# Down sums of three token blocks with stationary weights and transposed results, and V of the first 512 tokens moved ahead of wide Q and K projections

## The chip, the cores and the metric

The kernel runs on one core of a Trainium2 chip. The metric is the device time of one execution in microseconds (us), as a median over several runs. A profile, where one was taken, gives the *span*: from the first to the last instruction of the program on the core. The timed figure is longer than the span in every run here, by 1.73 to 2.14 us; that difference turns out to matter here.

Each run also lists the granted clock, the share of TensorE's full clock that the chip allowed.

## The reference, cut to what matters

```python
S, D, F, H, W, dil = 2048, 640, 1536, 32, 8, 2        # bf16 in and out
xn  = layernorm(x)
q, k, v = split(xn @ wqkv)                            # 640 -> 3 x 640
o   = local attention: each token looks at 8 tokens, 2 apart, per head of 20
out = x + o @ wo + ((xn @ w_gate) * (xn @ w_up)) @ w_down
```

## The kernel before: the parts that matter here

The kernel keeps everything of the 2048 tokens on the chip. Tokens come in 16 tiles of 128 and in 4 blocks of 512. `XNT` holds the normalized input with features on partitions. TensorE runs one long in-order list: Q and K of tiles 0 to 7, Q and K of blocks 2 and 3, V of blocks 0 to 3, gate and up ("GLU") of blocks 0 to 2, down of block 0, GLU of block 3, down of blocks 1 to 3. VectorE does LayerNorm, then the attention products, the softmax and the weighted sums of V, and leaves the attention output in `VO`. The down sum of a token adds 12 chunks of the GLU product (weights `WD`) and 5 chunks of `VO` (weights `WO`): 17 matmuls that accumulate in one PSUM bank.

Q and K of tiles 4 and 5 are computed one tile at a time (128 columns in a matmul), those of tiles 2, 3, 6 and 7 two tiles at a time (256 columns), because LayerNorm delivers tiles one after the other:

```python
def proj_part(which, t, ms, b, col):                  # 128 wide
    for c, m in [(c, m) for m in ms for c in range(NCH)]:
        o = PS[:, b, col + (m - ms[0]) * TS:col + (m - ms[0] + 1) * TS]
        l, x = wcols(which, c, m), XNT[:, c, t * TS:(t + 1) * TS]
        ...                                           # matmul, accumulating over c
def proj_wide(which, t0, m, b, col):                  # 256 wide
    o = PS[:, b, col:col + 2 * TS]
    ...
wide_pair(2)                                          # tiles 2, 3
for which, t in ((0, 4), (1, 4), (0, 5), (1, 5)):
    proj_part(which, t, (0, 1), b, 0); proj_part(which, t, (2, 3), b, 2 * TS); proj_part(which, t, (4,), ...)
wide_pair(6)                                          # tiles 6, 7
```

The down sum holds the activations stationary and streams the weights, 320 of the 640 output features at a time, so the result comes out with tokens on partitions and can be added to the output in memory as it is:

```python
def tail(t, nb):                                      # one tile of 128 tokens, one half of the features
    for i in range(n):                                # n = 12 + 5 = 17
        if i < NF: l, x = ht(j, i)[:, rows], WD[:, i, cols]                       # cols: 320 features
        else:      l, x = VO[:, i - NF, t * TS:(t + 1) * TS], WO[:, i - NF, cols]
        op("pe", ... matmul(PS[:, b, 0:wid], l, x, start=(i == 0), stop=(i == n - 1)))
    if t < TLAST:                                     # tiles 0 to 11: ScalarE evicts 640 features as fp16,
        ...                                           # and for every 2 tiles a DMA of the POOL queue adds them to `out`
    # tiles 12 to 15: VectorE adds x, plain DMA to `out`
```

## Time and profile before

| | |
|---|---|
| timed, 3 runs | 254.13 us median (253.92 to 254.18) |
| the profiled run | 376.75 us, span 375.0 us, granted clock 0.658 |

The profile fell into a throttled run, so its microseconds aren't those of the timed runs. The view of the cores says so:

```profile
core 0: 375.0 us, clock 0.658
```

The page of the same profile, its busy times and its clock line (tenths of full speed in 40 equal slices of the span):

```profile
PE 371.7 (99%) x1572; PEld 184.2 (49%) x1572; DVE 219.0 (58%) x255; ACT 114.5 (31%) x202; POOL 35.8 (10%) x44
...
PEclk8666666666666666666666666666666666666666
```

TensorE (PE) is busy all the time. What a slice of that time consists of is seen in the chain of waits, the work that ended last followed back. Its columns are start, length in us, and engine, tile and line with the number of instructions. L509, L489 and L474 are projections 256, 128 and 512 wide, L648 is GLU, L679 the down sums:

```profile
15.24 8.19 PE PS L509 x50
23.43 8.12 PE PS L489 x100
31.56 8.19 PE PS L509 x50
39.75 65.25 PE PS L474 x200
105.00 117.50 PE PS L648 x360
222.50 27.81 PE PS L679 x136
250.31 39.17 PE PS L648 x120
289.48 83.23 PE PS L679 x425
```

The pieces follow each other without a gap. Divide a length by its count and by the width: 8.12 us / 100 / 128 = 0.634 ns a column at a width of 128, 65.25 / 200 / 512 = 0.637 at a width of 512. At this clock a narrow matmul costs no more per column than a wide one, so this profile alone can't show what widening is worth.

The new gate of the change is on `VO`, which VectorE writes. In the timeline of the same profile (start, length, engine, line, operation), a 256-token piece of it takes from 236.60 to 247.36 us:

```profile
236.60 5.49 DVE L615 TENSOR_TENSOR PVB<-VO,ATB 128x10240 f16<-128x10240 bf16 x1
242.12 4.35 DVE L610 TENSOR_TENSOR PVB<-PVB 128x5120 f16<-128x5120 f16 x2
246.50 0.82 DVE L610 TENSOR_TENSOR VO<-PVB 128x1280 bf16<-128x1280 f16 x1
247.36 5.49 DVE L615 TENSOR_TENSOR PVB<-VO,ATB 128x10240 f16<-128x10240 bf16 x1
```

### The profile page before, as it was taken

The numbers are of one execution on the slowest core, as the hardware profiler recorded it, in microseconds if no ns is written. First come the engines' busy times: TensorE is split into PE (matmuls) and PEld (weight loads), VectorE is DVE, ScalarE is ACT, GpSimd is POOL, SyncE is SP. The second block draws the span as 40 slices with busy tenths as digits, with TensorE's granted clock in tenths as the row PEclk, the third lists the DMA queues.
The fourth block names the chain that finished last, engine by engine and source line by source line (L and its number), as shares of the span: only waits on it lengthen the run. The fifth ranks groups of instructions, "written<-read, shape, count | busy, mean of one in ns | idle before, by whom it ended". The sixth has DMA issues, their size and how long they took to land.

```text
span 375.0 us, 3825 instructions
## 1 busy us (share of the span) xinstructions
PE 371.7 (99%) x1572; PEld 184.2 (49%) x1572; DVE 219.0 (58%) x255; ACT 114.5 (31%) x202; POOL 35.8 (10%) x44
## 2 busy tenths in 40 slices
PE   8999999999999999999999999999999999999997
PEld 5998544444433333333333346553334556556555
DVE  5766899992017238967666432997846998000111
ACT  4544443333333344333333332113333001001000
POOL 0000012344000300111100000110000010010000
PEclk8666666666666666666666666666666666666666
DMA  7754696766100412453991000612000020220411
GB/s 218 217 115 84 181 361 148 129 120 120 20 0 2 92 20 82 149 107 71 251 344 18 0 1 0 180 80 35 2 0 0 0 37 0 35 37 0 72 35 35
DMA packets 25664, 31.83 MB, mean 85 GB/s; under 512 B 9872, under 2 KB 22160, under 8 KB 25616
## 3 DMA queue, kind: packets, MB, share of 16 engines
q1 hardware_dynamic: 19120, 22.16, 18.3%
q0 software_dynamic: 6240, 9.31, 15.7%
q8 instruction: 12, 0.20, 0.2%
q10 hardware_dynamic: 288, 0.13, 0.1%
q14 instruction: 4, 0.03, 0.0%
HBM read 14.42 MB, written 4.59 MB: 51 GB/s over the span
## 4 chain that ended last, share of the span: by engine, by line
PE 99%; DVE 0%; issue 0%
PE PS L648 42%; PE PS L679 30%; PE PS L474 17%; PE PS L509 4%; PE PS L502 2%; PE PS L489 2%; PE PS L452 1%; PE PS L433 0%; DVE FOUT L693 0%; DVE ZERO L296 0%; DVE EPSC L297 0%
## 5 line engine op out<-in xcount | busy, mean ns | idle before, releaser
L648 PE MATMUL PS<-XNT,WU 128*128 128x512 bf16 x240 | 87.3, 513 | 0.0
L648 PE MATMUL PS<-XNT,WG 128*128 128x512 bf16 x240 | 87.3, 513 | 0.0
L474 PE MATMUL PS<-XNT,WQKV 128*128 128x512 bf16 x200 | 65.4, 513 | 0.0
L679 PE MATMUL PS<-WD,HT 128*128 128x320 bf16 (+2 forms) x300 | 63.4, 382 | 0.0
L648 PEld LDWEIGHTS PS<-XNT,WG 128*128 128x128 bf16 x240 | 29.3, 122 | 48.8 <-issue 48.7
L648 PEld LDWEIGHTS PS<-XNT,WU 128*128 128x128 bf16 x240 | 29.0, 121 | 49.3 <-issue 49.3
L679 PEld LDWEIGHTS PS<-WD,HT 128*128 128x128 bf16 x300 | 35.5, 120 | 24.1 <-issue 0.9
L653 DVE TENSOR_TENSOR HT<-HT,USX 128x512 bf16<-128x512 bf16 x36 | 15.2, 422 | 54.8 <-ACT USX L650 54.8
L474 PEld LDWEIGHTS PS<-XNT,WQKV 128*128 128x128 bf16 x200 | 26.9, 135 | 38.0 <-issue 37.7
L615 DVE TENSOR_TENSOR PVB<-VO,ATB 128x10240 f16<-128x10240 bf16 x8 | 43.9, 5488 | 0.2
L650 ACT ACTIVATE USX<-PS 128x512 bf16<-128x512 f32 x48 | 28.6, 597 | 48.7 <-PE PS L648 47.7
L679 PE MATMUL PS<-WO,VO 128*128 128x320 bf16 (+2 forms) x165 | 38.8, 384 | 0.0
L610 DVE TENSOR_TENSOR PVB<-PVB 128x5120 f16<-128x5120 f16 (+1 forms) x16 | 34.5, 2155 | 0.3
L693 DVE TENSOR_TENSOR FOUT<-PS,XR 128x320 bf16<-128x320 f32 (+2 forms) x9 | 4.1, 454 | 51.7 <-PE PS L679 51.7
L650 ACT ACTIVATE HT<-PS 128x512 bf16<-128x512 f32 x36 | 21.5, 597 | 36.4 <-PE PS L648 36.4
L688 ACT ACTIVATE FACC<-PS 128x640 f16<-128x640 f32 x12 | 8.4, 703 | 73.3 <-PE PS L679 73.3
L543 POOL DMA_DIRECT2D LOG<-PE x24 | 21.9, 925 | 58.0 <-DMA LOG<-PE 58.0
L679 PEld LDWEIGHTS PS<-WO,VO 128*128 128x128 bf16 x165 | 19.7, 121 | 13.0
L703 POOL DMA_DIRECT2D out_dram<-FACC x6 | 7.1, 1186 | 141.9 <-ACT FACC L688 141.9
L532 DVE TENSOR_TENSOR PP<-QH,KH 128x2048 f16<-128x2048 bf16 x16 | 19.1, 1218 | 0.0
L532 DVE TENSOR_TENSOR TMP<-QH,KH 128x2048 f16<-128x2048 bf16 x16 | 19.0, 1218 | 0.0
L537 DVE TENSOR_TENSOR PP<-PP,TMP 128x4096 f16<-128x4096 f16 x8 | 18.3, 2289 | 0.2
(67 smaller groups left out, 250.6 us busy)
## 6 DMA issues: line engine op xcount, KB each, us to landing
PE<-PP POOLq DMA_DIRECT2D x8, 512.0 KB, 4.8
ATB<-LOG SPq DMA_DIRECT2D x8, 512.0 KB, 4.8
LOG<-PE POOLq DMA_DIRECT2D x24, 128.0 KB, 2.7
WG<-in_B_w_gate_dram SPq DMA_DIRECT2D x1, 1920.0 KB, 9.1
WU<-in_B_w_up_dram SPq DMA_DIRECT2D x1, 1920.0 KB, 15.8
WD<-in_B_w_down_dram SPq DMA_DIRECT2D x1, 1920.0 KB, 10.0
out_dram<-in_A_x_dram SPq DMA_DIRECT2D x1, 1920.0 KB, 9.1
out_dram<-FACC POOLq DMA_DIRECT2D x6, 320.0 KB, 4.8
```

The costliest lines, as they stand in the source:

```text
L474: op("pe", (lambda l, x, c: lambda e: e.matmul(PS[:, b, :], l, x, start=(c == 0), stop=(c == NCH - 1)))(l, x, c), r=[l, x], w=[PS[:, b, :] ...
L509: op("pe", (lambda l, x, c: lambda e: e.matmul(o, l, x, start=(c == 0), stop=(c == NCH - 1)))(l, x, c), r=[l, x], w=[o], name=f"pw{which}_ ...
L532: return (1.22, lambda: op("dve", lambda e: e.tensor_tensor(o, qw, kw, ALU.mult), r=[q, k], w=[o], name=f"prod{h}_{p}_{c}"))
L537: (2.3, lambda: op("dve", lambda e: e.tensor_tensor(a, a, b, ALU.add), r=[a, b], w=[a], name=f"psum{h}_{p}")),
L543: op("pool", lambda e: e.dma_start(o, i, accum_op=ALU.add), r=[o, i], w=[o], dma=True, name=name)
L610: return lambda: op("dve", lambda e: e.tensor_tensor(o, x, y, ALU.add), r=[x, y], w=[o], name=f"{name}_{b}")
L615: lambda: op("dve", lambda e: e.tensor_tensor(PVB[:], vw, aw, ALU.mult), r=[v, a], w=[PVB[:]], name=f"pv_{b}")),
L648: op("pe", (lambda l, x, c: lambda e: e.matmul(PS[:, b, :], l, x, start=(c == 0), stop=(c == NCH - 1)))(l, x, c), r=[l, x], w=[PS[:, b, :] ...
L650: op("act", lambda e: e.activation(o, PS[:, b, :], ACT.Copy), r=[PS[:, b, :]], w=[o], name=f"guev{which}_{m}_{j}")
L653: h_pending.append(lambda: op("dve", lambda e: e.tensor_tensor(h, h, o, ALU.mult), r=[h, o], w=[h], name=f"h{m}_{j}"))
L679: op("pe", (lambda l, x, i, b, wid: lambda e: e.matmul(PS[:, b, 0:wid], l, x, start=(i == 0), stop=(i == n - 1)))(l, x, i, b, wid), r=[l, ...
L688: op("act", (lambda o, i: lambda e: e.activation(o, i, ACT.Copy))(o, i), r=[PS[:, b - 1, :], PS[:, b, :]], w=[o], name=f"fin{t}")
```

## The change

The intent: the same columns in fewer, wider matmuls. For blocks 0 to 2 the down sum keeps the *weights* stationary and streams 512 tokens; the result then has features on partitions, so ScalarE writes it to `DT`, and a DMA of the sync queue transposes it into `FACC`, from where it is added to the output as before. Q and K of tiles 4 to 7 become one block of 512 columns. Since all four tiles must be there before the first such matmul, V of the first 512 tokens is put ahead of them, and V's weights are loaded earlier.

```diff
+    def down_t(j, d):                                   # block j, output features d*128 .. d*128+127
+        for i in range(n):                              # n = 17
+            if i < NF: l, x = WD[:, i, cols], ht(j, i)
+            else:      l, x = WO[:, i - NF, cols], VO[:, i - NF, toks]       # 512 tokens
+            op("pe", ... matmul(PS[:, b, :], l, x, start=(i == 0), stop=(i == n - 1)))
+        o = DT[:, (NCH * j + d) % 4]
+        op("act", ... activation(o, PS[:, b, :], ACT.Copy))
+        f = FACC[j][:, :, cols]
+        op("sp", lambda e: e.dma_start_transpose(f, o), r=[o], w=[f], dma=True)
+        ...                                             # after d == 4: two accumulating DMAs to `out`, 256 tokens each
     x_load2(8)
+    wqkv_load(2)                                        # V's weights, before: with the late loads
     x_load2(10)
...
-    wide_pair(2); (tiles 4 and 5 by proj_part); wide_pair(6)
+    (tiles 2 and 3 as before)
+    for m in range(NCH):
+        proj(2, m, 0)                                   # V of block 0
+    for m in (4, 0, 1, 2, 3):
+        for which in (0, 1):
+            proj(which, m, 1)                           # Q, K of block 1: 512 wide
...
     def add_dn(j):
+        if j < NJ - 1:
+            for d in range(NCH):
+                fill.append(("dn", 2 * j + 1, 3.67, lambda d=d: down_t(j, d)))
+            return
```

More of the change, by code (lines that the diff above doesn't have):

```diff
@@ L274, in build_kernel @@
     FOUT = sb("FOUT", [128, NFO, D])
-    FACC = sb("FACC", [128, NFO, D], FP16, at=place[0] - NFO * D * 2)
+    DT = sb("DT", [128, 4, JB], FP16, at=K.base[ATB[1].name] + NSB * W * SB * 2)
+    FACC = [sb(f"FACC{k}", [128, NJ, D], FP16, at=a) for k, a in
+            enumerate((place[0] - NFO * D * 2, K.base[ATB[0].name], K.base[ATB[0].name] + NJ * D * 2))]
     NUS = 7
@@ L343, in late_loads @@
         dma(MASK[0:128:4], MSK0[0:32], r=[MSK0[0:32]], w=[MASK[0:128:4]], name="mask")
-        wqkv_load(2)
         for T, src in ((WG, B_w_gate), (WU, B_w_up)):
@@ L482, in proj @@
            name=f"pev{which}_{m}_{j}")
-    def proj_part(which, t, ms, b, col):
-        for c, m in [(c, m) for m in ms for c in range(NCH)]:
-            o = PS[:, b, col + (m - ms[0]) * TS:col + (m - ms[0] + 1) * TS]
-            l, x = wcols(which, c, m), XNT[:, c, t * TS:(t + 1) * TS]
-            st, sp = c == 0, c == NCH - 1
-            op("pe", (lambda o, l, x, st, sp: lambda e: e.matmul(o, l, x, start=st, stop=sp))(o, l, x, st, sp),
-               r=[l, x], w=[o], name=f"pp{which}_{m}_{t}_{c}")
     def proj_tile(which, tiles, bm, at={}):
@@ L661, in build_kernel @@
     stores = []
-    fin_bank = [0]
+    def down_t(j, d):
+        flush_h(0)
+        b = bank()
+        n = NF + NCH
+        cols, toks = slice(d * TS, (d + 1) * TS), slice(j * JB, (j + 1) * JB)
+        for i in range(n):
+            if i < NF:
+                l, x = WD[:, i, cols], ht(j, i)
+            else:
+                l, x = WO[:, i - NF, cols], VO[:, i - NF, toks]
+            op("pe", (lambda l, x, i: lambda e: e.matmul(PS[:, b, :], l, x, start=(i == 0), stop=(i == n - 1)))(l, x, i),
+               r=[l, x], w=[PS[:, b, :]], name=f"dt{j}_{d}_{i}")
+        o = DT[:, (NCH * j + d) % 4]
+        op("act", lambda e: e.activation(o, PS[:, b, :], ACT.Copy), r=[PS[:, b, :]], w=[o], name=f"fin{j}_{d}")
+        f = FACC[j][:, :, cols]
+        op("sp", lambda e: e.dma_start_transpose(f, o), r=[o], w=[f], dma=True, name=f"oT{j}_{d}")
+        if d < NCH - 1:
+            return
+        for u in range(0, NJ, 2):
+            f2 = FACC[j][:, u:u + 2]
+            t = NJ * j + u
+            h = ohbm[t * TS:(t + 2) * TS, :].rearrange("(u p) n -> p u n", p=TS)
+            stores.append(op("pool", (lambda h, f2: lambda e: e.dma_start(h, f2, accum_op=ALU.add))(h, f2), r=[f2, ("out",)],
+                             w=[("out", t)], dma=True, name=f"oacc{t}"))
     def tail(t, nb):
@@ L680, in tail @@
                    r=[l, x], w=[PS[:, b, :]], name=f"dn{t}_{nb}_{i}")
-            if t < TLAST:
-                if nb == 0:
-                    fin_bank[0] = b
-                    continue
-                assert b == fin_bank[0] + 1
-                o = FACC[:, t % NFO, :].rearrange("p (n d) -> p n d", n=2)
-                i = PS[:, b - 1:b + 1, 0:wid]
-                op("act", (lambda o, i: lambda e: e.activation(o, i, ACT.Copy))(o, i),
-                   r=[PS[:, b - 1, :], PS[:, b, :]], w=[o], name=f"fin{t}")
-                continue
             o = FOUT[:, t % NFO, cols]
@@ L697, in tail @@
                 stores.append(dma(ohbm[t * TS:(t + 1) * TS, cols], o, r=[o], name=f"odma{t}_{c0}", eng=eng))
-        if nb == 1 and t < TLAST:
-            if t % 2 == 0:
-                return
-            f = FACC[:, (t - 1) % NFO:(t - 1) % NFO + 2, :]
-            d = ohbm[(t - 1) * TS:(t + 1) * TS, :].rearrange("(u p) n -> p u n", p=TS)
-            stores.append(op("pool", lambda e: e.dma_start(d, f, accum_op=ALU.add), r=[f, ("out",)], w=[("out", t)],
-                             dma=True, name=f"oacc{t}"))
-        elif nb == 1 and not last:
+        if nb == 1 and not last:
             f = FOUT[:, t % NFO, :]
@@ L772, in build_kernel @@
     tp = 11.9
-    def wide_pair(t0):
-        nonlocal tp
-        for g in range(5):
-            b = bank()
-            if g == 2:
-                proj_wide(0, t0, 4, b, 0)
-                proj_wide(1, t0, 4, b, 2 * TS)
-                part_evac(0, t0, 2, 4, 1, b, 0)
-                part_evac(1, t0, 2, 4, 1, b, 2 * TS)
-            else:
-                which, m = ((0, 0), (0, 2), None, (1, 0), (1, 2))[g]
-                proj_wide(which, t0, m, b, 0)
-                proj_wide(which, t0, m + 1, b, 2 * TS)
-                part_evac(which, t0, 2, m, 2, b, 0)
-            tp += 1.11
-            ln_pace(tp)
     bank_ring[:] = [5, 0, 2, 6, 7, 1, 3, 4]
-    wide_pair(2)
-    bm = bank()
-    for which, t in ((0, 4), (1, 4), (0, 5), (1, 5)):
+    for g in range(5):
         b = bank()
-        proj_part(which, t, (0, 1), b, 0)
-        proj_part(which, t, (2, 3), b, 2 * TS)
-        proj_part(which, t, (4,), bm, (2 * which + t - 4) * TS)
-        part_evac(which, t, 1, 0, 4, b, 0)
-        tp += 1.4
-        if (which, t) == (1, 5):
-            for u in (0, 1):
-                part_evac(u, 4, 2, 4, 1, bm, 2 * u * TS)
+        if g == 2:
+            proj_wide(0, 2, 4, b, 0)
+            proj_wide(1, 2, 4, b, 2 * TS)
+            part_evac(0, 2, 2, 4, 1, b, 0)
+            part_evac(1, 2, 2, 4, 1, b, 2 * TS)
+        else:
+            which, m = ((0, 0), (0, 2), None, (1, 0), (1, 2))[g]
+            proj_wide(which, 2, m, b, 0)
+            proj_wide(which, 2, m + 1, b, 2 * TS)
+            part_evac(which, 2, 2, m, 2, b, 0)
+        tp += 1.11
+        ln_pace(tp)
+    for m in range(NCH):
+        proj(2, m, 0)
+        tp += 1.08
         ln_pace(tp)
     bank_ring[:] = [6, 7, 2, 3, 4, 5, 0, 1]
-    wide_pair(6)
+    for m in (4, 0, 1, 2, 3):
+        for which in (0, 1):
+            proj(which, m, 1)
+            tp += 1.08
+            ln_pace(tp)
     ln_pace(1e9)
-    bank()
     k_seam()
@@ L812, in exp_preload @@
         op("act", lambda e: e.activation(DUM[:, 0:1], EPSC[:, 0:1], ACT.Exp), r=[EPSC[:]], w=[DUM[:]], name="exp_preload")
-    t_pe, t_dve = [30.3], [31.2]
+    t_pe, t_dve = [35.5], [31.8]
     fill, pos = [], [0]
@@ L823, in build_kernel @@
     QKB = len(fill)
-    for j in range(NJ):
+    for j in range(1, NJ):
         for m in range(NCH):
@@ L834, in add_dn @@
     def add_dn(j):
+        if j < NJ - 1:
+            for d in range(NCH):
+                fill.append(("dn", 2 * j + 1, 3.67, lambda d=d: down_t(j, d)))
+            return
         for t in range(4 * j, 4 * j + 4):
```

## The prediction

> **What bounds it.** TensorE. In the chain of waits PE holds 99% of the span, from 5.88 to 372.74 us without a gap; VectorE is busy 219.0 (busy table). But the profile was taken at a granted clock of 0.658 (cores view); the timed runs take 254. So count: about 575,000 columns stream through the array. In the chain a 512-wide projection takes 65.25/200 = 326 ns, a 256-wide 8.19/50 = 164 ns, a 128-wide 8.12/100 = 81 ns, the last down stretch (130,560 columns) 83.23 us: all 0.634 to 0.640 ns a column. At 0.658 of the clock, width costs nothing.
>
> At the full clock, an estimate: [...] plus 5.9 before the chain and 2.3 after it in the trace, plus 1.7 (376.75 timed against 375.0 span) = 253.4. Measured 254.13: about 0.7 us of waiting is left.
>
> **What the change does.**
> 1. Down of blocks 0 to 2: the columns are the same (17 x 5 x 512 = 4 x 17 x 640), but 255 matmuls for 408: -153 x 2.5 ns = -0.38 us.
> 2. Q and K of tiles 4 to 7: 50 matmuls 512 wide for 100 of 128 and 50 of 256: -100 x 2.5 ns = -0.25 us.
> 3. ScalarE: 15 evictions of 128x512 (597 ns in the groups) for 12 of 128x640 (703 ns): +0.5 us, hidden.
> 4. 15 DMA transposes on the sync queue (those of XNT land in 2.6 us), in stretches where the DMA is at 0 to 4 tenths: hidden. The last accumulate starts 18 us before the end.
> 5. V's weights load earlier (800 KB, 4.8 us to landing), before x of tiles 10 to 15: hidden.
> 6. VectorE's first product still follows the last LayerNorm; the last K comes at about 35 us: 0 to 1 us later.
> 7. Gates get coarser: all 512 tokens of VO are wanted at the 13th matmul of a block's first group (2.6 us in at full clock) (before: the first 256). VO of 256 tokens takes 10.8 us of VectorE (236.60 to 247.36), and pv of token block 1 ends with 4 of the 12 products of GLU block 2 still to come; so I estimate 3 to 6 us of slack at down 0, and 3 to 4 at downs 1 and 2. Probably no stall, but the danger.
>
> On the critical path: only 1 and 2, -0.63 us, perhaps 0.2 more at the GLU-to-down seams.
>
> **Predicted: 253.4 us, 8 in 10 between 252.6 and 254.6.** Faster by over 2%: 0.005; within 2%: 0.975; slower by over 2%: 0.02.
>
> **Right if** PE keeps 99% of the chain, matmul records fall by 253, the down line costs the same per column, and fast runs move -0.4 to -0.9 us. In a throttled profile the spans are equal within 0.3%. **Wrong if** PE shows idle before a first down group, released by VectorE (VO) or a HT product; if LayerNorm or XNT transposes come late because of V's weights; or if the transposes hold the sync queue and with it the last stores. If the 2.5 ns isn't there at full clock, the gain is zero.

For the columns and matmuls the sum needs 253.4 - 5.9 - 2.3 - 1.7 = 243.5 us, and points 1 and 2 need 2.5 ns a matmul. The author assumed both for the full clock; the profile of before, at 0.658, doesn't show them. The runs at a clock of 1.000 below do: 0.4167 ns a column (base) and 2.5 ns a matmul (base, glu_halves), so 575,000 columns and 1,480 matmuls take 239.6 + 3.7 = 243.3 us.

## The result, and the profile after

| | before | after |
|---|---|---|
| timed, 6 runs each | 254.16 us (253.89 to 254.24) | 253.81 us (253.68 to 253.98) |
| ratio | | 0.9989, 95% interval 0.9976 to 1.0002 |
| profiled run | throttled, see above | span 251.6 us, granted clock 1.000 |

A ratio here is the mean time of one kernel's runs over the mean of the other's runs of the same rounds, so it isn't quite the ratio of the medians. Executions over 1.5% slower than the fastest of the same kernel are left out of the means.

The direction and the range were met; the size was not. The prediction's mechanism gives 0.63 us, the medians moved 0.35 us and the ratio says 0.28 us. The range was wide beside that effect: the 254.16 us of before lie in it too, so meeting it says little. The interval of the ratio includes 1, so the times of this first set alone don't show a gain; the trace below does.

After was profiled at the full clock:

```profile
core 0: 251.6 us, clock 1.000
```

To compare like with like, the kernel before was profiled once more among the experiments below (the run "base": one run, so its state counts as unknown, but its granted clock is 1.000). This is its chain of waits, from the first 256-wide projection to the end:

```profile
13.21 5.46 PE PS L509 x50
18.67 5.58 PE PS L489 x100
24.25 5.46 PE PS L509 x50
29.71 43.17 PE PS L474 x200
72.88 77.70 PE PS L648 x360
150.58 18.47 PE PS L679 x136
169.05 25.90 PE PS L648 x120
194.95 55.48 PE PS L679 x425
250.43 0.02 issue
250.45 0.29 DVE FOUT L693
```

Now width does cost. 5.58 / 100 = 55.8 ns for 128 columns, 5.46 / 50 = 109.2 for 256, 18.47 / 136 = 135.8 for 320, 43.17 / 200 = 215.9 for 512 (GLU, as wide: 77.70 / 360 = 215.8). The line through 55.8 at 128 and 215.8 at 512 is 160.0 / 384 = 0.4167 ns a column plus about 2.5 ns a matmul. It gives 109.1 ns for 256 and 135.8 for 320, where the trace has 109.2 and 135.8.

The same view of the changed kernel, with the equal pieces in between left out. L503 is the 256-wide projection, L476 the 512-wide one, L642 GLU, L667 the new down sum, L697 the old one of block 3:

```profile
12.73 5.46 PE PS L503 x50
18.18 0.05 issue
18.24 10.74 PE PS L476 x49
28.98 0.05 issue
29.03 10.74 PE PS L476 x49
...
147.74 2.11 PE PS L642 x9
149.84 8.63 PE PS L667 x40
158.47 0.05 issue
158.53 9.66 PE PS L667 x44
168.19 1.08 PE PS L642 x5
...
230.78 18.53 PE PS L697 x153
249.33 0.29 DVE FOUT L701
```

The pieces of "49 and 0.05 issue" are not waits. In this trace 20 matmul records are missing (1299 matmuls, but 1319 weight loads), one of them in each such piece of 50, and 10.74 + 0.05 = 10.79 us is 50 x 215.8 ns. So TensorE has no gap in either kernel once the start is over.

From the 256-wide projection to the end of TensorE's work the two chains last 194.95 + 55.48 - 13.21 = 237.22 us and 230.78 + 18.53 - 12.73 = 236.58 us. The difference is 0.64 us, where 253 matmuls at 2.5 ns are 0.63.

The seam that the prediction feared most, GLU block 2 to down block 0, is this in the timeline of the changed kernel:

```profile
148.60 1.24 PE L642 MATMUL PS<-XNT,WU 128*128 128x512 bf16 x5
149.08 0.82 DVE L604 TENSOR_TENSOR VO<-PVB 128x1280 bf16<-128x1280 f16 x1
149.68 2.75 PE L667 MATMUL PS<-HT,WD 128*128 128x512 bf16 x12
152.27 1.24 PE L667 MATMUL PS<-VO,WO 128*128 128x512 bf16 x5
```

VectorE finishes the second piece of `VO` at 149.08 + 0.82 = 149.90 us, and TensorE first wants it at 152.27, 2.59 us after the first matmul of the group (149.68): 2.4 us to spare. The later blocks have more: the fourth piece is there at 183.3 and wanted at 196.5, the sixth at 207.3 and wanted at 214.9.

The transposes in the DMA views: name, queue, kind, count, and median us from issue to landing. First base, the kernel before at the full clock (the throttled profile has 2.6), then after:

```profile
XNT<-XNS SPq DMA_TRANSPOSE x12, 2.7
```

```profile
FACC<-DT SPq DMA_TRANSPOSE x15, 2.3
XNT<-XNS SPq DMA_TRANSPOSE x12, 3.6
```

The new transposes are as fast as expected. Those of LayerNorm became slower. A median of 12 hides which: followed one by one, the first three, issued from 14 to 17 us, land after 2.7, 2.6 and 2.6 us in base and after 5.3, 4.5 and 4.0 us in after, where the load of V's weights (800 KB, issued at 9.7 us, landing 7.8 us later) is in flight beside them. The kernel early_only below, which also loads V's weights early, has 5.4, 4.6 and 3.7 us, although its median is 2.7. "v_after" below shows what the delay would cost without V in between.

So inside the trace the whole forecast gain is there, and about half of it (0.28 to 0.35 of 0.63 us) is in the timed difference. Two terms are left to carry the rest: the start of the kernel, and the time outside the span.

### The profile page after: what moved, and what is told of

Its sections match the earlier page's. It is cut to its first block, busy times and chain, and to the rows that moved or that the text cites. A ratio compares the mean times of both kernels' runs of the same rounds, so it can differ in the third digit from the quotient of the medians.

```text
span 251.6 us, 3326 instructions
## 1 busy us (share of the span) xinstructions
PE 247.1 (98%) x1299; PEld 129.0 (51%) x1319; DVE 215.8 (86%) x255; ACT 114.6 (46%) x203; POOL 35.9 (14%) x44
## 4 chain that ended last, share of the span: by engine, by line
PE 96%; DMA 1%; SPq 1%; issue 1%; DVE 0%
PE PS L642 41%; PE PS L667 22%; PE PS L476 21%; PE PS L697 7%; PE PS L503 2%; PE PS L496 2%; DMA WQKV<-in_A_wqkv_dram 1%; SPq L295 1%; PE PS L435 0%; DVE FOUT L701 0%
## 5 line engine op out<-in xcount | busy, mean ns | idle before, releaser
L642 PE MATMUL PS<-XNT,WU 128*128 128x512 bf16 x237 | 59.0, 379 | 0.2
L642 PE MATMUL PS<-XNT,WG 128*128 128x512 bf16 x232 | 57.9, 379 | 0.4
L476 PE MATMUL PS<-XNT,WQKV 128*128 128x512 bf16 x245 | 53.7, 379 | 0.3
L476 PEld LDWEIGHTS PS<-XNT,WQKV 128*128 128x128 bf16 x250 | 29.4, 118 | 24.4
L642 PEld LDWEIGHTS PS<-XNT,WU 128*128 128x128 bf16 x240 | 23.5, 98 | 28.3
L642 PEld LDWEIGHTS PS<-XNT,WG 128*128 128x128 bf16 x240 | 23.5, 98 | 28.3
L670 ACT ACTIVATE DT<-PS 128x512 f16<-128x512 f32 x15 | 9.0, 597 | 43.8 <-PE PS L667 40.7
L667 PE MATMUL PS<-HT,WD 128*128 128x512 bf16 x118 | 27.4, 379 | 0.1
L667 PEld LDWEIGHTS PS<-HT,WD 128*128 128x128 bf16 x120 | 11.8, 98 | 14.1
L667 PE MATMUL PS<-VO,WO 128*128 128x512 bf16 x74 | 18.4, 379 | 0.0
L537 POOL DMA_DIRECT2D PE<-PP x8 | 7.9, 985 | 64.7 <-DVE PP L532 64.7
L483 ACT ACTIVATE VO<-PS 128x512 bf16<-128x512 f32 x20 | 11.9, 596 | 8.6 <-PE PS L476 8.4
```

What stands on the lines that cost most here:

```text
L476: op("pe", (lambda l, x, c: lambda e: e.matmul(PS[:, b, :], l, x, start=(c == 0), stop=(c == NCH - 1)))(l, x, c), r=[l, x], w=[PS[:, b, :] ...
L483: op("act", lambda e: e.activation(o, PS[:, b, :], ACT.Copy, scale=sc), r=[PS[:, b, :]], w=[o], name=f"pev{which}_{m}_{j}")
L537: op("pool", lambda e: e.dma_start(o, i, accum_op=ALU.add), r=[o, i], w=[o], dma=True, name=name)
L642: op("pe", (lambda l, x, c: lambda e: e.matmul(PS[:, b, :], l, x, start=(c == 0), stop=(c == NCH - 1)))(l, x, c), r=[l, x], w=[PS[:, b, :] ...
L667: op("pe", (lambda l, x, i: lambda e: e.matmul(PS[:, b, :], l, x, start=(i == 0), stop=(i == n - 1)))(l, x, i), r=[l, x], w=[PS[:, b, :]], ...
L670: op("act", lambda e: e.activation(o, PS[:, b, :], ACT.Copy), r=[PS[:, b, :]], w=[o], name=f"fin{j}_{d}")
```

## The experiments

Twelve kernels ran. The table has eleven of them (v_after lost clock and is told in its own place) and the runs of before beside them: means over the listed runs, all with a granted clock of 1.000; base, share4 and base_spare ran once, so their state counts as unknown. The span of each run is reported to 0.1 us. "Outside" is timed minus span. "Dense part" is from the start of the first 256-wide matmul to the start of the last matmul in the profiled run.

| kernel | runs | timed | span | outside | dense part |
|---|---|---|---|---|---|
| before, beside the first four | 9 | 254.13 | 252.33 | 1.80 | |
| before, beside the next four | 9 | 254.37 | 252.58 | 1.80 | |
| before, beside the next three | 11 | 254.28 | 252.49 | 1.79 | |
| before, beside the last | 9 | 254.15 | 252.37 | 1.78 | |
| after (first result) | 6 | 253.82 | 251.75 | 2.07 | 236.51 |
| after_again | 5 | 253.88 | 251.84 | 2.04 | 236.51 |
| down_only | 5 | 254.12 | 252.04 | 2.08 | 236.76 |
| early_only | 5 | 253.82 | 252.02 | 1.80 | 236.90 |
| glu_halves | 5 | 255.08 | 253.00 | 2.08 | 237.71 |
| base | 1 | 254.46 | 252.7 | 1.76 | 237.15 |
| share4 | 1 | 254.37 | 252.3 | 2.07 | 236.51 |
| base_spare | 1 | 254.09 | 252.3 | 1.79 | 237.15 |
| share_all | 5 | 254.13 | 252.04 | 2.09 | 236.51 |
| no_transpose (wrong values) | 6 | 253.69 | 251.88 | 1.80 | 236.51 |
| plain_copy (wrong values) | 5 | 253.93 | 251.84 | 2.09 | 236.51 |
| merged | 5 | 253.42 | 251.60 | 1.82 | 236.51 |

### First round: is it the count of matmuls, and which half gives the gain back?

**after_again**: no edit.

> The changed kernel unaltered, timed again beside the kernel before. Theory A (every matmul costs its columns at the full clock plus 2.5 ns, nothing else changed): 0.63 us less than before, ratio 0.9975. Theory B (the count of matmuls gives that, but some wait that is new at the start, at a GLU-to-down seam or at the end gives part of it back): about 0.3 us less as in the first runs, ratio 0.9988, and the trace shows the wait. Theory C (narrow and wide matmuls cost the same per column also at the full clock, no effect): ratio 1.000.

Measured: 253.93 us against 254.17, ratio 0.9991 (0.9978 to 1.0003). Theory C is out, since the dense part is 0.64 us shorter. The trace shows no new wait, so theory B is not right as it was put either.

**down_only**: the kernel before with `DT`, `FACC`, `down_t` and `add_dn` of the change.

> The kernel before with only the down part of the change (blocks 0 to 2 weights stationary, results through DMA transposes); start as before. Theory A: 153 matmuls fewer x 2.5 ns = 0.38 us less, ratio 0.9985. Theory B, if the giving back sits at the seams: 0.0 to 0.2 us less, with PE idle before the first VO matmul of a block. Theory C: 1.000.

Measured: 254.15 us, ratio 1.0000 (0.9988 to 1.0013). The dense part fell by 0.39 us as theory A says, but the timed result hardly moved. No TensorE idle at the seams.

**early_only**: the kernel before with the early part alone (V ahead, Q and K 512 wide).

> The kernel before with only the early part of the change (V of the first 512 tokens ahead, Q and K of tiles 4 to 7 512 wide, V's weights loaded earlier); down sums as before. Theory A: 100 matmuls fewer x 2.5 ns = 0.25 us less, ratio 0.9990. Theory B, if the giving back sits at the start: 0.0 us or slower, with PE idle in the first 35 us. Theory C: 1.000.

Measured: 253.77 us, ratio 0.9986 (0.9973 to 1.0000). The dense part fell by 0.25 us, exactly the count of matmuls; the timed result fell by more, but its interval includes 0.25 us.

**glu_halves**: the changed kernel, each GLU matmul cut in two on the same weights.

```diff
-        for c in range(NCH):
-            l, x = T[:, c, m * 128:(m + 1) * 128], XNT[:, c, j * JB:(j + 1) * JB]
+        for h0 in (0, 256):
+            for c in range(NCH):
+                l, x = T[:, c, m * 128:(m + 1) * 128], XNT[:, c, j * JB + h0:j * JB + h0 + 256]
```

> The changed kernel with each 512-wide GLU matmul cut into two of 256 on the same weights: 480 matmuls more, the same columns. Theory A: 480 x 2.5 ns = 1.2 us more than the changed kernel, so about 0.6 us more than before, ratio 1.0023; 256-wide start to start 109.2 ns against 215.8 for 512. Theory C: no more than the changed kernel, ratio to before 0.9985 to 1.000. If weight loads were what narrow matmuls pay for, more than 2 us more.

Measured: 255.06 us, ratio to before 1.0038 (1.0025 to 1.0050). Dense part 237.71 - 236.51 = 1.20 us longer for 480 matmuls more: 2.5 ns each, and not the more than 2 us of the rival with weight loads. The mean span grew by 1.16 us over that of after_again. The price of a matmul is settled for these runs: 2.5 ns at the widths seen here, 128 to 512, at a granted clock of 1.000. Against before the run is 0.95 us slower in the mean, where 0.6 was forecast: that forecast lacked what comes next.

What follows from this round is in the column "outside". The spans fell by 0.49 (after_again), 0.29 (down_only) and 0.31 us (early_only), near to the forecast 0.63, 0.38 and 0.25. But the kernels with the new down sum pay 2.04 to 2.08 us outside their span, and those without it 1.80. These 0.26 us are what the timed result of the change lacks, and no run strays from this: over single runs the one group is at 1.73 to 1.84, the other at 2.03 to 2.14.

The rest is the start. TensorE's list up to the first 256-wide matmul is the same in all kernels, and so are the loads that it waits for, yet the start of that matmul falls between 12.5 and 13.3 us over the profiles, whichever kernel it is. In the profile of after the chain goes through the load of Q's and K's weights (3.63 us of waiting for `WQKV`), in that of base through the load of x (4.26 us for `XST`). The spans of one kernel's timed runs scatter too, by 0.3 us in after (251.6 to 251.9) and by 0.5 us in before beside after_again (252.1 to 252.6), which is as large as the effect.

### Second round: semaphores

The new down sum adds 15 DMAs, and in this kernel each DMA has a semaphore of its own: 126 instead of 111. 0.26 us / 15 = 17 ns, about what a semaphore instruction takes in this trace (EVENT_SEMAPHORE: a median of 17 ns over 106 of them in after), so I suspected that semaphores are paid for after the end (theory D).

**base**: the kernel before, for its profile.

> The kernel before unaltered, for a profile at the full clock (the one of before was throttled). Theory A: from the first 256-wide matmul to the last matmul 0.63 us longer than in the changed kernel (236.51 us there), so 237.1 us; time outside the span 1.80 us, as its other fast runs have it, against 2.06 us in the changed kernel.

Measured: dense part 237.15 us, as said; outside 1.76 us.

**share4**: the 15 transposes on four semaphores.

```diff
-        op("sp", ... dma_start_transpose(f, o), ..., name=f"oT{j}_{d}")
+        k = NCH * j + d
+        if k < 4: t_sems.append(nc.alloc_semaphore(f"oT{k}"))
+        op("sp", ... dma_start_transpose(f, o), ..., event=(t_sems[k % 4], 16 * (k // 4 + 1)))
```

> The changed kernel, its 15 result transposes signalling on 4 semaphores with rising counts instead of on 15 of their own (115 semaphores in all instead of 126, the kernel before has 111); nothing else differs. Theory D (what gave back 0.26 us is paid outside the span, about 17 ns for each semaphore the program uses, 0.26/15): timed minus span falls from 2.06 to about 1.87 us. Rival E (the transposes or their descriptors are what is paid for outside the span): stays at 2.06 us.

Measured: 2.07 us outside. A miss for theory D.

**base_spare**: the kernel before with 15 unused semaphores.

> The kernel before with 15 semaphores more that are allocated and never used (126, as the changed kernel has). Theory D if what counts is the allocation: timed minus span rises from 1.80 to 2.06 us. Theory D if what counts is use, or rival E: stays at 1.80 us.

Measured: 1.79 us outside: allocation costs nothing.

**share_all**: every DMA takes over the semaphore of an earlier one whose end its issuer has already waited for; 33 semaphores.

```diff
+            if X.dma:
+                for p in pool[E]:
+                    if kn.get(p[0], 0) >= p[1]:      # this engine already knows that it is done
+                        p[1] += 16
+                        break
+                else:
+                    p = [nc.alloc_semaphore(f"dma{self.n_dma}"), 16]
+                    ...
+                X.event = (p[0], p[1])
```

> The changed kernel in which every DMA reuses the semaphore of an earlier DMA of the same queue whose end its issuer has already waited for: 33 semaphores instead of 126, no wait added or taken away. Theory D: timed minus span falls by 93 x 17 ns = 1.6 us, from 2.06 to about 0.45 us, span unchanged at 251.8; time about 252.3 us, ratio to before 0.9925. Rival E: 2.06 us and 253.9 us, ratio 0.999.

Measured: 254.07 us, ratio 0.9990 (0.9976 to 1.0003), outside 2.09 us. With 93 semaphores fewer nothing changed. Theory D falls: neither the number allocated nor the number used costs time here.

### Third round: the transposes, and why V goes first

**no_transpose** (values wrong): ScalarE writes the untransposed result straight into `FACC`.

```diff
-        o = DT[:, (NCH * j + d) % 4]
-        op("act", ... activation(o, PS[:, b, :], ACT.Copy))
         f = FACC[j][:, :, cols]
-        op("sp", ... dma_start_transpose(f, o))
+        op("act", ... activation(f, PS[:, b, :] seen as 4 x 128, ACT.Copy))
```

> The changed kernel without its 15 result transposes: ScalarE writes each 512-wide result straight into the buffer that is added to the output (values wrong on purpose: 128x128 pieces stay untransposed). 15 DMAs and their semaphores fewer, all else equal. Theory D fell with the semaphore runs. Theory E (the transposes, or 15 DMAs of any kind on that queue, are paid for outside the span): timed minus span 1.80 us, span as in the changed kernel, time 253.6 us or 0.63 us below before, ratio 0.9975. Rival F (something else of the down part is paid for, such as the longer ScalarE or the regrouped accumulates): stays 2.06 us, ratio 0.999.

Measured: 253.51 us, ratio 0.9979 (0.9967 to 0.9991), outside 1.80 us, mean span 0.61 us under that of before. This is what the prediction described: the whole gain arrives once the 15 DMAs are gone. So they, with the waits that they bring to other engines, are what is paid for, and rival F as it was put (ScalarE's evictions or the accumulates) is out.

**plain_copy** (values wrong): `dma_start` in place of `dma_start_transpose`.

> The changed kernel with 15 plain DMA copies of the same 128 KB in place of the 15 transposes, same queue, same waits (values wrong on purpose). Theory E1 (it is the transposing itself): timed minus span 1.80 us. Theory E2 (15 more DMAs of any kind on the sync queue): 2.06 us. Span as in the changed kernel either way.

Measured: 253.92 us, ratio 0.9987 (0.9975 to 0.9999), outside 2.09 us. It isn't the transposing: 15 plain copies on the sync queue, with the same waits, cost the same.

**v_after**: V of block 0 behind Q and K of block 1 again.

```diff
-    for m in range(NCH):
-        proj(2, m, 0)
     for m in (4, 0, 1, 2, 3):
         for which in (0, 1):
             proj(which, m, 1)
             ...                                         # pacing of LayerNorm, here and in the other loops
+    for m in range(NCH):
+        proj(2, m, 0)
```

> The changed kernel with V of the first 512 tokens put behind Q and K of tiles 4 to 7 again, these still 512 wide. In the changed kernel's trace the transpose of tile 7 is issued at about 18.7 us and these land in 3.6 us, while TensorE would want it at 18.24 us: PE idle of 3 to 4 us there, ratio to before about 1.011 to 1.013. Rival (the order of V is worth nothing, the wide matmuls alone make the gain): ratio 0.999.

Measured: 256.96, 258.56, 259.50 and 261.29 us; ratio of the runs that count as fast 1.016 (1.0128 to 1.0193), two of these three at a clock of 0.993. The rival is out; V's place is what lets the wide Q and K go without a stall. The one run that kept a clock of 1.000 took 256.96 us, 1.0105 of before's mean and 3.1 us over after_again: about the forecast stall (that run has no profile). The ratio is larger because the other three runs lost clock besides (0.987 to 0.993), which the forecast did not have. The profile is one of these, and is used for the mechanism alone. First the list of waits (engine, tile, line, released by: total, times, longest), then the busy times in stretches of the span (PE, weight loads, DVE, ACT and POOL, then granted clock, DMA share, GB/s):

```profile
PE PS L476 <- DMA XNT<-XNS: 5.5, 1, 5.5
```

```profile
12.00:18.00 6.00, 6.00 (x63) 5.88 (x60) 5.97 (x23) 4.91 (x14) 0.00 (x0) 1.00 1.49 284
18.00:24.00 6.00, 0.49 (x3) 0.16 (x2) 2.55 (x8) 0.78 (x2) 0.00 (x0) 0.74 0.70 157
24.00:30.00 6.00, 6.00 (x21) 2.59 (x20) 2.64 (x10) 2.34 (x6) 0.00 (x0) 0.69 0.34 78
30.00:40.00 10.00, 10.00 (x48) 5.46 (x47) 8.57 (x24) 6.24 (x14) 0.00 (x0) 1.00 0.54 99
```

TensorE stands still for 5.5 us, from 18.15 to 23.66 us, until the transposes of LayerNorm land. The granted clock averages 0.74 and 0.69 in the two stretches from 18 to 30 us, and 1.00 before and after them. Work in that time is slower: in the timeline the first four matmuls after the stall take 1.90 us, four as wide in after (at 147.74 us) 1.03 us. A clock at half from about 20.9 us, 2.7 us after TensorE's last matmul, to about 27.7 us would give both averages, which is an estimate. By it the last 4.0 us of the half clock fell on work, an estimated loss of 2.0 us; with the 5.5 us of standing still that is 7.5 of the 7.65 us by which the dense part (244.16 us here) is longer than in after.

### Fourth round: fewer DMAs for the same bytes

**merged**: two transposes for each block, the first four column groups in one DMA and the fifth in another; `DT` and `FACC` are laid out for that, and the accumulates are cut by columns (still two for each block).

```diff
+        if d < 4: o = flat.rearrange("p (u d c) -> p u d c", u=NJ, d=4)[:, :, d]
+        else:     o = DT[:, 0, :].rearrange("p (u c) -> p u c", u=NJ)
+        op("act", ... activation(o, PS[:, b, :] seen as 4 x 128, ACT.Copy))
+        if d < 3: return
+        c0, wid, i = (0, 512, flat) if d == 3 else (512, TS, DT[:, 0, :])
+        f = facc[:, NJ * c0:NJ * (c0 + wid)]
+        op("sp", ... dma_start_transpose(f seen as (k, 128), i))
+        h = ohbm[toks, c0:c0 + wid].rearrange("(u p) n -> p u n", p=TS)
+        op("pool", ... dma_start(h, f, accum_op=ALU.add))
```

> The changed kernel with two result transposes for each block (four column groups at once, then the fifth) instead of five, so 6 DMAs where there were 15, moving the same bytes; still 6 accumulates, cut by columns. Right values. Theory E2 as a count (each further DMA of the sync queue costs about 17 ns outside the span): timed minus span 1.80 + 6 x 0.017 = 1.90 us, time about 253.75 us, ratio 0.998. Rival G (it goes with the bytes moved or with there being such a stage at all): 2.06 us, ratio 0.9985 to 0.999. Span as in the changed kernel in both; if the larger transposes or the later accumulates delay anything, the span is longer.

Measured: 253.42 us (253.24 to 253.64) against 254.08, ratio 0.9969 (0.9955 to 0.9983); values right. Outside 1.82 us, span 0.77 us shorter in the mean, dense part the same. Its DMA view:

```profile
FACC<-DT SPq DMA_TRANSPOSE x6, 5.7
```

The rival G is out: the same bytes go through the same stage. But the count with a price of 17 ns each, which wanted 1.90 us, is out as well: 6 more DMAs cost 0.02 us, 15 cost 0.26. Either it is a step, somewhere between 6 and 15 more DMAs, or it goes with something else that the 15 bring and the 6 do not (see the table below). This version beats the kernel before by about 0.3%. It was not timed beside the changed kernel: 253.42 us in the mean against 253.82 and 253.88 are from different rounds.

What it may be is hinted at in the traces, but not shown. The pages list two DMA queues of the kind "instruction": q8 (10 packets in after, of 16,384 bytes each) and q14, whose largest packets have 8,192 bytes. From the packets of each profile, this is when the last 8,192-byte packet falls, beside the number of instructions in the profile (waits and DMA issues included) of SyncE (SP), GpSimd (POOL) and ScalarE (ACT):

```
kernel         SP   POOL   ACT   end of span   last 8,192-byte packet at
base           78    56    246      252.7          253.8
base_spare     78    56    246      252.3          253.4
early_only     78    56    244      252.2          253.3
no_transpose   78    56    243      251.6          252.7
merged         84    56    248      251.8          251.6
after          93    61    254      251.6          239.3
after_again    93    61    254      251.9          240.5
down_only      93    61    256      252.1          240.7
share4         93    61    254      252.3          239.8
share_all      93    61    254      252.1          239.9
plain_copy     93    61    254      251.7          239.8
glu_halves     93    61    254      253.2          240.6
v_after        93    61    254      259.2          246.5
```

The groups by this time are the groups by "outside", without an exception: 1.73 to 1.84 us where the last of these packets is at the end, 2.03 to 2.14 where it comes 11 to 13 us before it. That would fit a step, but it is a correlation: no run shows that these packets cost time outside the span, and the profile doesn't say which engine they belong to.

There is a rival that no run tests. The 15 DMAs bring 5 more waits of POOL (before its accumulates) and some of ScalarE (before it may write `DT` again); no_transpose and merged have none of those 5 of POOL, and every kernel of the slower group has all of them. A price of 52 ns for each of the 5 would fit all runs too, without a step. No run moved these packets alone or added these waits alone, so the cause stays open.

## Why the prediction was right or wrong, point by point

- *"What bounds it: TensorE."* Right. The chain at full clock shows TensorE without a gap from the first wide projection to its last matmul in both kernels.
- *The 2.5 ns per matmul at full clock.* Right, though only assumed when it was written. Base shows 55.8, 109.2, 135.8 and 215.9 ns for widths of 128, 256, 320 and 512; glu_halves, with 480 more matmuls, 1.20 us more.
- *Point 1, -0.38 us, and point 2, -0.25 us.* Right in the dense part of the trace: 0.39 and 0.25 us, 0.64 together. The "perhaps 0.2 more" at the seams did not come, because there was no wait at the seams to cover.
- *Points 3 to 6, hidden.* Right as far as the span goes: no new wait in the traces. Point 5 was closer than it was put: the first transposes of LayerNorm take 4.0 to 5.3 us to land instead of 2.6 to 2.7 at the same clock, and only V's five groups in between keep TensorE from waiting (v_after).
- *Point 7, the gates.* Right that nothing stalls. "3 to 6 us" at down 0 is 2.4 us in the trace; "3 to 4" at down 2 is 7.5 us, and at down 1 it is 13 us.
- *"Fast runs move -0.4 to -0.9 us."* Wrong: -0.35 us in the medians, -0.28 us in the ratio; on the second set -0.24 us. The step that failed is the term "plus 1.7 (376.75 timed against 375.0 span)", which the sum carried over unchanged from before to after. It is 1.80 us in before and 2.06 us in after. So point 4 was wrong in one word: the 15 DMAs are hidden in the span, but not in the time. no_transpose shows that they, with the waits that they bring, are the cause, share_all and base_spare that their semaphores are not, plain_copy that the transposing is not, and merged that it is not a price for each DMA. Whether it is a step somewhere between 6 and 15 added DMAs or goes with the five waits of POOL stays open.
- *"About 0.7 us of waiting is left."* Only roughly: at full clock the dense part has no waiting; what remained was the start, whose end scatters between 12.5 and 13.3 us from run to run.

## What to carry to other kernels

When an engine is full, count exactly: here the columns at 0.4167 ns, plus 2.5 ns for each matmul, gave to a tenth of a microsecond what the rearrangement was worth in the dense part (0.63 us counted, 0.64 measured). But take both figures from a profile at the same clock: the throttled one, with 0.634 to 0.640 ns a column at every width, hid the very cost that the change removes. Hold timed minus span apart for every run before looking for a lost gain inside the trace; here 40% of the gain went there, and a version with 6 instead of 15 added DMAs got it back. If a wide matmul needs several inputs that arrive one by one, put work that is already ready in front of it: in the profile of v_after the stall that this avoids cost twice, 5.5 us as idle time and about 2.0 us as lost clock.
